# QKV row 0's mean from two partial sums, and a new order of the first loads

## The chip, the cores and the metric

The kernel runs on one core of one Trainium2 chip. Its time is the device time of one execution in microseconds (us), and the median of several runs is compared. A core has TensorE (PE, matrix products into PSUM; its weight loads are listed as PEld), VectorE (DVE), ScalarE (ACT), GpSimd (POOL) and SyncE (SP). Each engine works through its own instructions in order; they wait for each other through semaphores. SyncE and ScalarE each have a queue through which they start DMA transfers; in the profile ScalarE's is q10 and SyncE's q1.

## The reference, cut to what matters

One layer norm feeds two branches, whose results are added to the input: a dilated sliding-window attention (32 heads of 18, 8 keys at distance 2), and a gated feed-forward network.

```python
x = A_x                                    # 1 x 2048 x 576, bf16
xn = _layernorm(x, axis=-1)                # (x - mean) / sqrt(var + 1e-5)
return x + _A_ref(xn, A_wqkv, A_wo) + _B_ref(xn, B_w_gate, B_w_up, B_w_down)

# _A_ref: qkv = x @ wqkv (576 x 1728); for each position s and head h
#   logits over keys s, s-2, ..., s-14 (masked below 0), softmax, weighted sum of v; then @ wo
# _B_ref: (silu(x @ w_gate) * (x @ w_up)) @ w_down, with 4608 hidden columns
```

## The kernel before, in words

The 2048 tokens are 16 row tiles ("rows" 0 to 15) of 128 tokens each, one token to a partition. The kernel has three stretches, one after the other on TensorE: the QKV products of all 16 rows (the first 60 us or so), then for four blocks of four rows the gate and up products (`g_pair`, `g_evac`) and the down and output products (`d_half`, `d_out`). The attention's elementwise work runs on VectorE beside it, from a queue of pieces with written costs (`Filler`). Nothing of this is touched by the change; what it touches is the beginning.

A product needs its operand transposed, with the 576 columns on partitions. They are five slices of 128, the last one padded from 64 columns to 128 by repeating columns 512 to 575. For rows 0 and 1 TensorE itself transposes (`transp_pe`, against an identity matrix), slice by slice into PSUM, and `copy_pt` copies the result to SBUF. `xT_of` names the place: for row 0 the scratch `xcT` (tile PP), for other rows their columns of `xnT`. From row 2 on `transp_halves` or a transposing DMA does it.

The weights `wqkv` come as four slices of 128 rows (`load_w` 0 to 3, 442 KB each) and a rest of 64 rows (`load_w` 4, two transfers of half the columns each); x rows 0 to 3 one at a time (`load_x`, 147 KB each), and later rows in blocks of four. In the profile they go by the tiles that share their memory: x rows are `wd<-in_A_x_dram`, weight slices `hT<-in_A_wqkv_dram`.

Row 0 is treated in a way of its own, so that TensorE need not wait for its variance. Its columns are centered only (`ln_center`, x minus mean, on VectorE; `ln_center_pad`, the padding, on GpSimd); the product is made from that, and the division by the standard deviation is done when the product leaves PSUM (`p_evac` with r = 0 multiplies by `rstd`). The mean comes from `ln_stats(0)`: two BN_STATS over half a row each (`ln_half`) and an aggregate (`ln_aggr`), which give mean and variance. For the feed-forward branch row 0 is also normalized in full later on (`ln_apply(0)` into `xn0`, transposed by a DMA, `transp_dma(0)`). Row 1 is normalized right away: `ln_stats(1)`, `ln_sqrt(1)` on ScalarE, `ln_recip(1)` and `ln_apply(1)` on VectorE, with a padding on GpSimd.

The schedule is written by hand: each engine executes in the order in which the lines at the end (L477 on) issue its instructions. For the first rows this order is, on TensorE: eleven warm-up matmuls on constants (`warm_pe(10, 1)`; ten of 512 columns and one of 128), row 0's five transposes, row 0's products with slices 0, 1 and half of 2 (`p_whole(0, t, ...)`, four matmuls of 432 columns to a slice), row 1's first three transposes, the rest of slice 2, row 1's last two transposes, row 1's products with slice 0 (into the banks `u`), row 0's slice 3 and rest (`p_row0_rest`), and then `p_row(1, ...)`, into which row 2's transposes are inserted.

PSUM has eight banks. `warm_ps` (also `pt1`), `pa`, `pb` and the four banks `t` take seven; of `u` the first is the eighth, and the others take over `pt1`, `pa` and `pb` after their contents have been copied out.

On SyncE's queue a transfer waits for an earlier one where it reuses its semaphore: eight are used in turn, so that the ninth load waits for the landing of the first.

The lines that matter most for the steps below:

```python
477    warm_pe(10, 1)
479    ln_stats(0)
481    ln_center(0, 0, P)
489    ln_stats(1)
492    ln_recip(0)
493    ln_apply(0)
504    copy_pt(nc.vector.tensor_copy, 1, (2,), pa)
```

Of the kernel before, what the change touches and what calls it, by code (L numbers as in the profile page):

```python
# [10 lines left out]
f32 = mybir.dt.float32  # L11
ACT = mybir.ActivationFunctionType
ALU = mybir.AluOpType
AX = mybir.AxisListType
# [3 lines left out]
P = 128  # L18
H, DH, W, DIL = 32, 18, 8, 2
D = H * DH  # L20
HALF = D // 2
# [4 lines left out]
DPAD = KT * P  # L26
# [44 lines left out]
def kernel(  # L71
# [11 lines left out]
    nc = tc.nc  # L83
# [9 lines left out]
    const = ctx.enter_context(tc.tile_pool(name="const", bufs=1))  # L93
# [19 lines left out]
    PP = big.tile([P, 2, RT * D], bf16, name="PP")  # L113
# [30 lines left out]
    def load_x(eng, j):  # L144
        eng.dma_start(xc_b[0][:, j:j + 1, :], x_v[:, j:j + 1, :])

    def load_w(eng, kt):
        if kt < 4:
            eng.dma_start(wqkv[:, kt, :], A_wqkv[kt * P:(kt + 1) * P, :])
        else:  # L150
            for i in range(2):
                eng.dma_start(wqkvr[64 * i:64 * i + 64, :], A_wqkv[4 * P:D, 2 * G * i:2 * G * (i + 1)])

    load_x(nc.scalar, 0)
    load_x(nc.sync, 1)
    load_w(nc.scalar, 1)
    load_w(nc.sync, 0)
    make_identity(nc, ident[:])
    load_w(nc.sync, 2)
    load_x(nc.sync, 2)  # L160
# [8 lines left out]
    pt1 = wp[:].bitcast(bf16)  # L169

    def warm_pe(n, m):
        one = lambda shape: nc.const_aps.tensor(1.0, shape, bf16)
        for i in range(n):
            nc.tensor.matmul(wp[:].rearrange("p (a b) -> p a b", b=P), one([P, P]), one([P, 4, P]),  # L174
                             start=True, stop=True)
        for i in range(m):
            nc.tensor.matmul(wp[:, 0:P], one([P, P]), one([P, P]), start=True, stop=True)  # L177
# [18 lines left out]
    def new_ps(name):  # L196
        return ps.tile([P, 512], f32, name=name, tag="ps")


    ln = {}  # L200

    def ln_open(c):
        mv = lns.tile([P, 4, 2], f32, name="mv")
        rstd = lns.tile([P, 4], f32, name="rstd")
        ln[c] = (xc_b[c], xn_b[c % 2], mv, rstd)

    sums = {}

    def ln_half(r, k):
        c, j = divmod(r, 4)  # L210
        xc, xn, mv, rstd = ln[c]
        if k == 0:
            sums[r] = lns.tile([P, 2, 6], f32, name="stats")
        nc.vector.bn_stats(sums[r][:, k, :], xc[:, j, k * HALF:(k + 1) * HALF])  # L214

    def ln_aggr(r):
        c, j = divmod(r, 4)
        nc.vector.bn_aggr(ln[c][2][:, j, :], sums[r][:].rearrange("p c s -> p (c s)"))

    def ln_stats(r, n=1):  # L220
        for i in range(r, r + n):
            ln_half(i, 0)
            ln_half(i, 1)
            ln_aggr(i)

    def ln_sqrt(r, n=1):
        c, j = divmod(r, 4)
        xc, xn, mv, rstd = ln[c]
        nc.scalar.activation(rstd[:, j:j + n], mv[:, j:j + n, 1], ACT.Sqrt, bias=eps_t[:], scale=1.0)

    def ln_recip(r, n=1):
        c, j = divmod(r, 4)
        rstd = ln[c][3]
        nc.vector.reciprocal(rstd[:, j:j + n], rstd[:, j:j + n])

    def ln_apply(r):
        c, j = divmod(r, 4)
        xc, xn, mv, rstd = ln[c]
        dst = xn[:, j] if r else xn0
        nc.vector.tensor_scalar(dst[:, 0:D], xc[:, j], mv[:, j, 0:1], rstd[:, j:j + 1],  # L240
                                op0=ALU.subtract, op1=ALU.mult)
        if r < 2:
            nc.gpsimd.tensor_scalar(dst[:, D:DPAD], xc[:, j, 512:D], mv[:, j, 0:1], rstd[:, j:j + 1],
                                    op0=ALU.subtract, op1=ALU.mult)
        else:
            nc.vector.tensor_copy(dst[:, D:DPAD], dst[:, 512:D])

    def ln_center(r, lo=0, hi=D):
        c, j = divmod(r, 4)
        xc, xn, mv, rstd = ln[c]  # L250
        nc.vector.tensor_scalar(xn[:, j, lo:hi], xc[:, j, lo:hi], mv[:, j, 0:1], None, op0=ALU.subtract)

    def ln_center_pad(r):
        c, j = divmod(r, 4)
        xc, xn, mv, rstd = ln[c]
        nc.gpsimd.tensor_scalar(xn[:, j, D:DPAD], xc[:, j, 512:D], mv[:, j, 0:1], None, op0=ALU.subtract)

    def transp_pe(r, kts, pt):
        c, j = divmod(r, 4)
        xn = ln[c][1]  # L260
        for i, kt in enumerate(kts):
            nc.tensor.transpose(pt[:, i * P:(i + 1) * P], xn[:, j, kt * P:(kt + 1) * P], ident[:])  # L262

    def xT_of(r):
        return xcT if r == 0 else xnT[:, :, r * P:(r + 1) * P]

    def copy_pt(eng, r, kts, pt):
        eng(xT_of(r)[:, kts[0]:kts[-1] + 1, :],
            pt[:, 0:len(kts) * P].rearrange("p (k t) -> p k t", t=P))

    def new_pt():
        return ps.tile([P, 8 * P], bf16, name="pt", tag="ps")

    def transp_halves(r):


        c, j = divmod(r, 4)
        xn = ln[c][1]
        pt = [new_ps("pt") for half in range(2)]
        for kt in range(KT):  # L280
            for half in range(2):
                rows = slice(64 * half, 64 * half + 64)
                nc.tensor.matmul(pt[half][:, kt * 64:(kt + 1) * 64], xn[rows, j, kt * P:(kt + 1) * P],  # L283
                                 ident[rows, rows], start=True, stop=True)
        for half, eng in enumerate((nc.scalar.copy, nc.vector.tensor_copy)):
            lo = r * P + 64 * half
            eng(xnT[:, :, lo:lo + 64], pt[half][:, 0:KT * 64].rearrange("p (k t) -> p k t", t=64))  # L287
# [11 lines left out]
    def p_mm(t, g, kt, half, r, start, stop):  # L299
        rows = slice(0, P) if half is None else slice(64 * half, 64 * half + 64)  # L300
        return nc.tensor.matmul(t[g][:, 0:G], xT_of(r)[rows, kt, :], w_at(g, kt, rows),  # L301
                                start=start, stop=stop)

    def p_whole(r, t, kt, gs=range(NG)):
        for g in gs:
            p_mm(t, g, kt, None, r, kt == 0, False)
# [6 lines left out]
    def fence_after(mm):  # L313
        f = nc.gpsimd.engine_nop()
        tc.add_manual_dep(f.ins, mm.ins.name, SYNC, reason="first half done")
        return f

    def fence_before(mm, f):
        tc.add_manual_dep(mm.ins, f.ins.name, SYNC, reason="banks change row tiles")

    def p_row(r, between=None, at=(0, 1), t=None):


        done = t is not None
        t = t or [None] * NG
        fence = {}
        for swap in range(2):
            for i in range(2):
                for kt in (0, 1, 2, 3) if swap else (0, 4, 1, 2, 3):
                    if done and kt == 0:  # L330
                        continue
                    for half in range(2):
                        g = i + 2 * (half ^ swap)
                        if t[g] is None:
                            t[g] = new_ps("qkv_ps")
                        mm = p_mm(t, g, kt, half, r, swap == 0 and kt == 0, swap == 1 and kt == 3)
                        if swap == 0 and kt == 3 and half == 1:
                            fence[i] = fence_after(mm)
                        if swap and kt == (1 if done else 0) and half == 0:
                            fence_before(mm, fence[i])  # L340
                    if swap and (i, kt) == at and between is not None:
                        between()
        return t
# [130 lines left out]
    def turn(r):  # L474
        return lambda: transp_halves(r)

    warm_pe(10, 1)  # L477
    ln_open(0)
    ln_stats(0)
    ln_center_pad(0)  # L480
    ln_center(0, 0, P)
    ln_sqrt(0)
    pa, pb = new_pt(), new_pt()
    transp_pe(0, (0,), pa)
    ln_center(0, P, D)
    transp_pe(0, range(1, KT), pb)
    copy_pt(nc.scalar.copy, 0, (0,), pa)
    copy_pt(nc.scalar.copy, 0, (1, 2), pb)
    ln_stats(1)
    ln_sqrt(1)  # L490
    copy_pt(nc.scalar.copy, 0, (3, 4), pb[:, 2 * P:])
    ln_recip(0)
    ln_apply(0)
    ln_recip(1)
    ln_apply(1)

    t = [new_ps("qkv_ps") for g in range(NG)]
    p_whole(0, t, 0)
    p_whole(0, t, 1)
    p_whole(0, t, 2, (0, 1))  # L500
    transp_pe(1, (0, 1), pt1)
    transp_pe(1, (2,), pa)
    copy_pt(nc.scalar.copy, 1, (0, 1), pt1)
    copy_pt(nc.vector.tensor_copy, 1, (2,), pa)
    p_whole(0, t, 2, (2, 3))
    transp_pe(1, (3, 4), pb)
    copy_pt(nc.scalar.copy, 1, (3, 4), pb)
    u = [None] * NG
# [11 lines left out]
    load_gu(0)  # L520
    transp_dma(0)

    p_row(1, turn(2), (0, 2), u)
    ln_aggr(3)
    p_evac(1, u, (0, 1, 2), dve=(1, 2))
    ln_sqrt(3)
# [8 lines left out]
    t = p_row(2, turn(3))  # L535
# [6 lines left out]
    t = p_row(3, turn(4))  # L542
# [10 lines left out]
    for r in range(4, R):  # L553
        t = p_row(r)
# [92 lines left out]
    for tt in range(NTT):  # L647
# [29 lines left out]
        for sub in range(0, RT, 2):  # L677
            t, fence = {}, {}
# [36 lines left out]
```

## Time and profile before

| what | us |
|---|---|
| three runs | 503.34, 503.36, 504.67 (median 503.36) |
| the profiled execution | 503.82 |
| its span | 502.0 |
| PE busy | 498.1 (99%) |
| VectorE busy | 329.0 (66%) |
| ScalarE busy | 200.5 (40%) |
| GpSimd busy | 2.6 (1%) |
| the QKV matmuls (L301) in the chain | 11% of the span |
| the warm-up matmuls (L174) in the chain | 1% of the span |

The profile is of one execution. Its times are counted from the start of the span. A line of the timeline gives the start, the length, the engine (SPq and ACTq are the parts that issue DMAs), the line of the kernel, the operation, the tiles and shapes, the number of instructions merged in the line, and in brackets how long the engine had been idle and what ended that. A matmul's length includes its way through the array, so matmuls overlap; the pace is the distance between starts. The chain is followed back from the last instruction of the program, at each step to what released it, and its lines give start, length and what ran.

### The profile page before, as it was taken

To read this page: it belongs to the slowest core of one execution; us is meant where nothing else is said; L and a number is where in the kernel's file an instruction comes from. 1 tells how busy PE (TensorE), PEld (TensorE's weight loads), DVE (VectorE), ACT (ScalarE), POOL (GpSimd) and SP (SyncE) were. 2 spreads that over 40 slices of the span, in tenths; PEclk is the share of its full clock that TensorE was granted. 3 is DMA by queue.
4 is the path that set the end of the run, shared out by engine and by line. 5 is a ranking of instruction groups with operands and counts; after the bars stand their busy time and mean duration, and the time that the engine had idled before them with its cause. 6 is when DMAs were issued, how large, how long until landed. Compare 5 with 4: busy or idle time off the path is not lost.

```text
span 502.0 us, 13267 instructions
## 1 busy us (share of the span) xinstructions
PE 498.1 (99%) x5795; PEld 330.5 (66%) x5795; DVE 329.0 (66%) x478; ACT 200.5 (40%) x415; POOL 2.6 (1%) x9
## 2 busy tenths in 40 slices
PE   9999999999999999999999999999999999999997
PEld 4666655555799755555899655555999555557996
DVE  5888598898999698999898139995980222221001
ACT  4756657644400255554300445557000454553000
POOL 2000000000000000000000000000000000000000
PEclk9999999999999999999999999999999999999999
DMA  8889988789921045536621154465600335453100
GB/s 313 219 206 228 307 280 280 220 273 309 233 82 61 25 136 193 191 106 225 161 69 43 29 185 146 139 189 157 136 25 14 100 114 178 155 177 38 29 14 25
DMA packets 77186, 75.42 MB, mean 150 GB/s; under 512 B 22708, under 2 KB 72528, under 8 KB 77128
## 3 DMA queue, kind: packets, MB, share of 16 engines
q1 hardware_dynamic: 76840, 73.98, 49.7%
q8 instruction: 45, 0.74, 0.6%
q10 hardware_dynamic: 288, 0.59, 0.4%
q14 instruction: 13, 0.11, 0.1%
HBM read 58.76 MB, written 5.90 MB: 129 GB/s over the span
## 4 chain that ended last, share of the span: by engine, by line
PE 99%; DVE 0%; issue 0%
PE g_ps L601 56%; PE d_ps L630 32%; PE qkv_ps L301 11%; PE warm_ps L174 1%; PE pt L262 0%; DVE ot L644 0%; PE pt L283 0%; PE warm_ps L262 0%; PE warm_ps L177 0%
## 5 line engine op out<-in xcount | busy, mean ns | idle before, releaser
L601 PE MATMUL g_ps<-xnT,gu 64*128 64x512 bf16 x2592 | 280.4, 376 | 0.0
L601 PEld LDWEIGHTS <-gu 64*128 64x128 bf16 x2592 | 147.7, 94 | 131.3
L612 ACT ACTIVATE sg<-g_ps 128x512 bf16<-128x512 f32 x144 | 87.3, 606 | 156.6 <-PE g_ps L601 156.6
L630 PE MATMUL d_ps<-wd,hT 64*128 64x288 bf16 x2304 | 146.9, 283 | 0.0
L630 PEld LDWEIGHTS <-hT 64*128 64x128 bf16 x2304 | 131.3, 94 | 10.5
L614 DVE TENSOR_TENSOR hT<-sg,uc 128x512 bf16<-128x512 bf16 x144 | 60.0, 418 | 93.8 <-ACT uc L613 93.6
L613 ACT CAST uc<-g_ps 128x512 bf16<-128x512 f32 x144 | 85.2, 592 | 0.0
L414 DVE TENSOR_REDUCE PP<-PP 128x64 f32<-128x1152 bf16 x64 | 84.9, 1345 | 0.4
L301 PE MATMUL qkv_ps<-hT,xnT 64*128 64x432 bf16 (+1 forms) x536 | 50.2, 343 | 0.0
L409 DVE TENSOR_TENSOR PP<-QO,Kr 128x2304 bf16<-128x2304 bf16 (+1 forms) x35 | 43.5, 1249 | 7.2 <-DMA Kr<-hT 6.9
L642 DVE TENSOR_TENSOR ot<-d_ps,xr 128x288 bf16<-128x288 f32 x30 | 12.3, 451 | 51.1 <-PE d_ps L630 51.1
L441 DVE TENSOR_TENSOR PP<-Vr,A 128x2304 bf16<-128x2304 bf16 (+1 forms) x35 | 43.2, 1250 | 0.4
L301 PEld LDWEIGHTS <-xnT 64*128 64x128 bf16 (+1 forms) x536 | 30.1, 94 | 18.5 <-ACT xnT L287 0.4
L446 DVE TENSOR_TENSOR PP<-PP 128x2304 bf16<-128x2304 bf16 x24 | 32.5, 1353 | 0.3
L612 ACT ACT_TABLE_LOAD x5 | 6.4, 1283 | 47.3 <-PE g_ps L601 47.2
L630 PE MATMUL d_ps<-wo,xnT 64*128 64x288 bf16 x288 | 23.4, 283 | 0.0
L363 ACT CAST hT<-qkv_ps 128x288 bf16<-128x288 f32 (+2 forms) x58 | 21.2, 428 | 0.5 <-DMA kv_d<-hT 0.5
L630 PEld LDWEIGHTS <-xnT 64*128 64x128 bf16 x288 | 16.4, 94 | 1.2
L434 ACT ACTIVATE PP<-PP 128x1024 f32<-128x1024 f32 x4 | 4.2, 1057 | 31.2 <-DVE PP L430 31.2
L644 ACT CAST ot<-d_ps 128x288 bf16<-128x288 f32 x1 | 0.4, 399 | 38.8 <-PE d_ps L630 38.8
L363 ACT CAST QO<-qkv_ps 128x432 bf16<-128x432 f32 (+1 forms) x30 | 12.3, 410 | 7.4 <-PE qkv_ps L301 7.4
L214 DVE BATCH_NORM_STATS2 stats<-wd 128x6 f32<-128x288 bf16 x32 | 12.9, 444 | 2.9 <-DMA wd<-in_A_x_dram 2.6
(53 smaller groups left out, 91.3 us busy)
## 6 DMA issues: line engine op xcount, KB each, us to landing
gu<-in_B_w_gate_dram SPq DMA_DIRECT2D x36, 512.0 KB, 3.8
gu<-in_B_w_up_dram SPq DMA_DIRECT2D x36, 512.0 KB, 5.1
wd<-in_B_w_down_dram SPq DMA_DIRECT2D x9, 576.0 KB, 6.0
kv_d<-hT SPq DMA_DIRECT2D x5, 576.0 KB, 6.4
gu<-in_B_w_gate_dram SPq DMA_DIRECT2D x36, 64.0 KB, 4.7
gu<-in_B_w_up_dram SPq DMA_DIRECT2D x36, 64.0 KB, 4.4
xr<-in_A_x_dram SPq DMA_DIRECT2D x8, 288.0 KB, 5.1
out_dram<-ot SPq DMA_DIRECT2D x16, 144.0 KB, 1.8
```

What stands on the lines that cost most here:

```text
L214: nc.vector.bn_stats(sums[r][:, k, :], xc[:, j, k * HALF:(k + 1) * HALF])
L301: return nc.tensor.matmul(t[g][:, 0:G], xT_of(r)[rows, kt, :], w_at(g, kt, rows), start=start, stop=stop)
L363: (nc.vector.tensor_copy if n in dve else nc.scalar.copy)(*parts[n])
L409: nc.vector.tensor_tensor(prod[:, a:b], QO[:, RT * tt + a:RT * tt + b, :], Kr[:, s:s + b - a, :], op=ALU.mult)
L414: nc.vector.tensor_reduce(L[:, w, rs], prod[:, rs].rearrange("p r (h d) -> p r h d", d=DH), axis=AX.X, op=ALU.add)
L441: nc.vector.tensor_tensor(dst[:, a:b], Vr[:, s:s + b - a, :].rearrange("p r (d h) -> p r d h", h=H), A[:, w, a:b].unsqueeze(2).to_broadcas ...
L446: nc.vector.tensor_tensor(dst, acc, pv, op=ALU.add)
L601: mm = nc.tensor.matmul(ring_ps[j][b][:], gu[rows, slot, k, fc], xnT[rows, kt, tok], start=(swap == 0 and kt == 0), stop=(swap == 1 and kt ...
L612: nc.scalar.activation(sg[:], t[0][:], ACT.Silu)
L613: nc.scalar.copy(uc[:], t[1][:])
L614: nc.vector.tensor_tensor(hT[:, ch * FC + j, :], sg[:], uc[:], op=ALU.mult)
L630: mm = nc.tensor.matmul(t[sub][h][:, 0:HALF], a[rows], w[rows, h * HALF:(h + 1) * HALF], start=(swap == 0 and n == 0), stop=(swap == 1 and ...
```

## The change

- The first loads change place. x row 0 goes on SyncE's queue and weight slice 0 alone on ScalarE's; SyncE's queue then has x row 1, slices 1 and 2, x row 2, slices 3 and 4 and x row 3. Before, ScalarE's queue had x row 0 and slice 1; SyncE's began with x row 1 and slice 0.
- Row 0's mean is computed by itself (`ln_mean0`): ScalarE copies the first half of the row to scratch and takes along the sum, VectorE sums the second half, and a one-column operation on VectorE adds the two and multiplies by 1/576. `ln_center` and `ln_center_pad` read this mean.
- Row 0's statistics (`ln_half(0, 0)`, `ln_half(0, 1)`, `ln_aggr(0)`, `ln_sqrt(0)`) are issued later, in between and after those of row 1, and `ln_recip(0)` and `ln_apply(0)` come after `ln_apply(1)`.
- ScalarE's third copy of row 0's transposes comes ahead of `ln_sqrt(1)`.
- One 512-column warm-up matmul is dropped (nine instead of ten).
- Three of the four matmuls of row 0's slice 2 come ahead of row 1's transposes, instead of two.
- The copy of row 1's slices 0 and 1 is split in two.
- Row 2's transposes come one step (two matmuls) earlier in `p_row(1, ...)`.

```diff
--- before.py
+++ after.py
@@ -151,10 +151,10 @@
             for i in range(2):
                 eng.dma_start(wqkvr[64 * i:64 * i + 64, :], A_wqkv[4 * P:D, 2 * G * i:2 * G * (i + 1)])
 
-    load_x(nc.scalar, 0)
+    load_x(nc.sync, 0)
+    load_w(nc.scalar, 0)
     load_x(nc.sync, 1)
-    load_w(nc.scalar, 1)
-    load_w(nc.sync, 0)
+    load_w(nc.sync, 1)
     make_identity(nc, ident[:])
     load_w(nc.sync, 2)
     load_x(nc.sync, 2)
@@ -205,6 +205,14 @@
         ln[c] = (xc_b[c], xn_b[c % 2], mv, rstd)
 
     sums = {}
+    part = const.tile([P, 2], f32, name="part")
+    mean = const.tile([P, 1], f32, name="mean")
+
+    def ln_mean0():
+        xc = ln[0][0]
+        nc.scalar.activation(PP[:, 1, 0:HALF], xc[:, 0, 0:HALF], ACT.Copy, accum_out=part[:, 0:1])
+        nc.vector.tensor_reduce(part[:, 1:2], xc[:, 0, HALF:D], axis=AX.X, op=ALU.add)
+        nc.vector.tensor_scalar(mean[:], part[:, 0:1], part[:, 1:2], 1.0 / D, op0=ALU.add, op1=ALU.mult)
 
     def ln_half(r, k):
         c, j = divmod(r, 4)
@@ -248,12 +256,12 @@
     def ln_center(r, lo=0, hi=D):
         c, j = divmod(r, 4)
         xc, xn, mv, rstd = ln[c]
-        nc.vector.tensor_scalar(xn[:, j, lo:hi], xc[:, j, lo:hi], mv[:, j, 0:1], None, op0=ALU.subtract)
+        nc.vector.tensor_scalar(xn[:, j, lo:hi], xc[:, j, lo:hi], mean[:], None, op0=ALU.subtract)
 
     def ln_center_pad(r):
         c, j = divmod(r, 4)
         xc, xn, mv, rstd = ln[c]
-        nc.gpsimd.tensor_scalar(xn[:, j, D:DPAD], xc[:, j, 512:D], mv[:, j, 0:1], None, op0=ALU.subtract)
+        nc.gpsimd.tensor_scalar(xn[:, j, D:DPAD], xc[:, j, 512:D], mean[:], None, op0=ALU.subtract)
 
     def transp_pe(r, kts, pt):
         c, j = divmod(r, 4)
@@ -474,35 +482,39 @@
     def turn(r):
         return lambda: transp_halves(r)
 
-    warm_pe(10, 1)
+    warm_pe(9, 1)
     ln_open(0)
-    ln_stats(0)
+    ln_mean0()
     ln_center_pad(0)
     ln_center(0, 0, P)
-    ln_sqrt(0)
     pa, pb = new_pt(), new_pt()
     transp_pe(0, (0,), pa)
     ln_center(0, P, D)
     transp_pe(0, range(1, KT), pb)
     copy_pt(nc.scalar.copy, 0, (0,), pa)
     copy_pt(nc.scalar.copy, 0, (1, 2), pb)
+    copy_pt(nc.scalar.copy, 0, (3, 4), pb[:, 2 * P:])
     ln_stats(1)
     ln_sqrt(1)
-    copy_pt(nc.scalar.copy, 0, (3, 4), pb[:, 2 * P:])
+    ln_half(0, 0)
+    ln_recip(1)
+    ln_apply(1)
+    ln_half(0, 1)
+    ln_aggr(0)
+    ln_sqrt(0)
     ln_recip(0)
     ln_apply(0)
-    ln_recip(1)
-    ln_apply(1)
 
     t = [new_ps("qkv_ps") for g in range(NG)]
     p_whole(0, t, 0)
     p_whole(0, t, 1)
-    p_whole(0, t, 2, (0, 1))
+    p_whole(0, t, 2, (0, 1, 2))
     transp_pe(1, (0, 1), pt1)
     transp_pe(1, (2,), pa)
-    copy_pt(nc.scalar.copy, 1, (0, 1), pt1)
+    copy_pt(nc.scalar.copy, 1, (0,), pt1)
+    copy_pt(nc.scalar.copy, 1, (1,), pt1[:, P:])
     copy_pt(nc.vector.tensor_copy, 1, (2,), pa)
-    p_whole(0, t, 2, (2, 3))
+    p_whole(0, t, 2, (3,))
     transp_pe(1, (3, 4), pb)
     copy_pt(nc.scalar.copy, 1, (3, 4), pb)
     u = [None] * NG
@@ -520,7 +532,7 @@
     load_gu(0)
     transp_dma(0)
 
-    p_row(1, turn(2), (0, 2), u)
+    p_row(1, turn(2), (0, 1), u)
     ln_aggr(3)
     p_evac(1, u, (0, 1, 2), dve=(1, 2))
     ln_sqrt(3)
```

## The prediction

> **What bounds the kernel now.** I read the page's busy table first, then its chain, then the same chain in order of time, and last the first 14 us as a timeline, engine by engine.
>
> ```profile
> PE 498.1 (99%) x5795; PEld 330.5 (66%) x5795; DVE 329.0 (66%) x478; ACT 200.5 (40%) x415; POOL 2.6 (1%) x9
> PE 99%; DVE 0%; issue 0%
> ```
>
> TensorE (PE) is busy for 99% of the span and is 99% of the chain that ended last, so a microsecond by which its stream shifts is a microsecond of the time. The change touches the first 13 us alone. The chain there:
>
> ```profile
> 0.76 4.42 PE warm_ps L174 x10
> 5.18 0.11 PE warm_ps L177
> 5.29 0.21 PE pt L262
> 5.50 0.02 issue
> 5.52 0.61 PE pt L262 x4
> 6.13 2.25 PE qkv_ps L301 x10
> 8.37 0.11 PE warm_ps L262 x2
> 8.48 0.06 PE pt L262
> 8.54 0.37 PE qkv_ps L301 x2
> 8.91 0.11 PE pt L262 x2
> 9.02 3.86 PE qkv_ps L301 x32
> ```
>
> The eleven warm-up matmuls compute nothing: PE's real work starts with row 0's transposes at 5.2. From the first QKV matmul (starts 6.06) it hardly pauses, so I follow one milestone: the start of slice 3 of row 0 (`p_whole(0, t, 3)`), 9.69 now. By the timeline nothing after it waits for long (0.10 us at 10.42, 0.13 us at 13.6), so a shift there reaches the end. What leads up to it, in the timeline of all engines:
>
> ```profile
> 3.81 0.82 DVE L214 BATCH_NORM_STATS2 stats<-wd 128x6 f32<-128x288 bf16 x2 [2.63 <-DMA wd<-in_A_x_dram]
> 4.66 0.21 DVE L218 BATCH_NORM_AGGREGATE mv<-stats 128x2 f32<-128x12 f32 x1
> 4.90 0.56 DVE L251 TENSOR_SCALAR wd<-wd,mv 128x128 bf16<-128x128 bf16 x2
> 5.54 0.27 ACT L268 COPY PP<-pt 128x128 bf16<-128x128 bf16 x1 [0.34 <-PE pt L262]
> 6.13 0.43 SPq L165 DMA_DIRECT2D wd<-in_A_x_dram  x1
> 8.58 0.23 DVE L268 COPY xnT<-pt 128x128 bf16<-128x128 bf16 x1 [1.11 <-PE pt L262]
> ```
>
> Row 0 lands at 3.81 (VectorE had waited 2.63 us for it). Statistics take to 4.90, where the centering starts. The copy of the first transposed slice ends at 5.81 and the transposes stream until 5.92, but the first QKV matmul waits until 6.06 for weight slice 0; SyncE's second block load, which waits for that same slice, goes at 6.13. At 8.58 the last row shows slack: VectorE has idled 1.11 us when it copies row 1's third slice out of PSUM.
>
> **Part 1, the loads.** DMA queues q10 (ScalarE) and q1 (SyncE), between 2.4 and 2.8 us, then between 3.6 and 4.8:
>
> ```profile
> q10 hardware_dynamic: 57, 0.06, 50.2%
> q1 hardware_dynamic: 53, 0.06, 42.6%
> ...
> q1 hardware_dynamic: 75, 0.26, 53.5%
> q10 hardware_dynamic: 73, 0.25, 50.0%
> ...
> wd<-in_A_x_dram ACTq DMA_DIRECT2D x1, 144.0 KB, 3.1
> wd<-in_A_x_dram SPq DMA_DIRECT2D x1, 144.0 KB, 3.2
> ```
>
> With both queues loaded, each gets the same number of packets, whatever their size. Packets are rows: 1152 bytes of x (51 ns of an engine each: q1's 42.6% of 16 engines' 0.4 us over 53 packets), 3456 of a weight slice (about 136 ns, in the same way from the second pair). Now x row 0 shares the engines with x row 1: 8 packets of each on each of 16 engines, 16 x 51 = 0.82 us. After the change it shares them with slice 0: 8 x (51 + 136) = 1.50 us, 0.68 more. It also moves to SyncE's queue, whose row took 3.2 us instead of 3.1. Row 0's landing goes from 3.81 to 0.72 + 3.2 + 0.68 = 4.60. Bounds: 3.9 (the smaller packets lose nothing) and 4.75. Slice 0 gains: it finishes beside row 0, near 4.6 instead of 6.02, and its wait at 6.06 is gone. Slices 2 to 4 have the same bytes ahead of them as before. SyncE issues two loads more and one less; at 0.44 to 0.6 us an issue its eighth, which waits for row 0's landing (3.80 now), starts at 4.6, with over 1 MB still queued, so nothing runs dry. ScalarE issues one load less (0.46), hidden before the landing.
>
> **Part 2, the mean.** Removed ahead of the centering: two BN_STATS and the aggregate, 3.81 to 4.90 = 1.10 us. Added, on two engines side by side: VectorE's reduction of 288 values, 0.34 us by the row of 1152 in 1345 ns, 0.44 by BN_STATS over the same 288; ScalarE's copy of 288, 0.43 us (CAST of 288) to 0.50 (ACTIVATE of 288), and reading out its sum, which no row shows: nothing, or 0.20 (the one-column ACTIVATE `warm`, nearest), up to 0.29 (the one-column ACTIVATE `rstd`). I take 0.43 + 0.20 + 0.04 for the handover, then one column on VectorE, 0.19 start to start (reciprocal to its user, 6.85 to 7.04). Centering starts 0.86 after the landing (0.65 to 1.05), 0.24 sooner than 1.10. Call its start C: 4.60 + 0.86 = 5.46 against 4.90.
>
> **Part 3, PE up to the first QKV matmul.** The first transpose starts C + 0.31 = 5.77 and the matmuls C + 1.03 = 6.49, against 6.06: 0.43 late. The dropped warm-up (0.43) ends PE's warm-up at 4.66; PE then idles 1.1 us instead of 0.13, and the drop gains nothing.
>
> **Part 4, the new order on VectorE and ScalarE.** Distances start to start from the trace of before: bn(1) at C + 0.48 and + 0.85, aggregate + 1.32, then half of row 0's statistics + 1.45. ScalarE's three copies + 0.63, + 1.26, + 1.56, and sqrt(1) + 1.87. recip(1) + 2.22, apply(1) + 2.41, second half of row 0 + 2.76, aggregate + 3.24, sqrt(0) + 3.48, recip(0) + 3.83, apply(0) + 4.03, and only then the copy of row 1's third slice, + 4.38 to + 4.60. That copy frees the PSUM bank `pa`; by the trace of before the second matmul of row 1's slice 0 (9.14) is the one that waits for a VectorE semaphore, and this copy is the only candidate I see. It now starts at C + 4.65 = 10.11 instead of 9.14. On ScalarE row 1's copies stand behind sqrt(0): C + 3.75 to + 4.0 for the first, within that bound; splitting it costs 0.17 of ScalarE, also within. Moving one matmul (0.18) ahead of row 1's transposes is an exchange on PE; they would be reached near 8.7, when row 1 (C + 2.84 = 8.3) and its pad on POOL (0.64 more, needed by the last two alone) are there.
>
> So the milestone moves from 9.69 to 10.11 + 3 x 0.183 = 10.66: **+0.97 us**, of which 0.56 is C and the rest the order. Row 2's transposes are moved two matmuls up; VectorE has row 2 ready at C + 4.38 + 2.40 = 12.25, PE comes at 12.72 + 0.97 - 0.18 = 13.5, no wait. The transposing DMA of row 0 waits for apply(0), and its pad on POOL, at about 10.3 now; it went at 11.6, behind SyncE's gu loads: hidden.
>
> **The sum.** The profiled execution took 503.82 (span 502.0 and 1.82 around it), 0.46 above the median of the runs, so it is 504.79 there, and 503.36 + 0.97 = **504.3** for the median. (0.3%, 1.5 us, is about what a measurement of this kernel can tell from no change.)
>
> **Rivals.**
> *The clock comes later (slower).* Early matmuls run at half the later pace: the 512-column warm-ups 0.43 us apart, QKV matmuls of 432 columns 0.36 apart at 6.38, and 0.183 apart from 6.9 on, 6 us after PE began. If PE's new idle stretch makes that run-up start over at 5.77, the fast pace comes at 11.8: eleven matmuls at 0.36 (6.49 to 10.45), three transposes 0.32, one matmul, two transposes 0.21, and most of row 1's slice 0 slow bring the milestone to 12.26: +2.57, 505.9. For it: the idle stretch is over 1 us, where the run-up of before had three pauses of 0.1 to 0.2. Against it: the granted clock of the windows reads 1.00 throughout and shows no such state. It decides once the fast pace comes after about 8 us. [...]
> *Row 0 isn't delayed.* The small packets pass the large ones: landing 3.92, C = 4.78, milestone 9.98: +0.29, 503.65. With the cheapest mean (0.65) it is +0.08. Against it: the equal packet counts.
> *Faster by over 0.3%.* PE would have to start QKV at 4.6, the very end of its warm-ups, and VectorE's chain of part 4 not to hold it. Against it: 1.4 us is all there is between warm-up's end and 6.06. At best, without the `pa` wait and the delay, about 503.1.
>
> **How the numbers follow.** My forecast 0.54 (503.9 to 504.7); no delay 0.16; clock 0.28; faster 0.02. Of the forecast a tenth lies past 504.87, from the upper bounds of landing and mean. Slower 0.33, same 0.65, faster 0.02. Range: from 503.2, below the undelayed row, to 505.9, the clock rival.
>
> **What would show it.** Row 0's landing by VectorE's first wait: 4.6, or 3.9. Centering 0.86 after it. First QKV matmul at 6.5. Row 1's third copy after apply(0), near 9.8, and PE's wait for it. The spacing of QKV matmuls before and after 7 us. I am wrong if the two queues don't alternate, if another operation than that copy frees the bank, or if the clock's run-up restarts.

## The result, and the profile after

The changed kernel takes 505.47 us (median of 8 executions, 504.56 to 507.34), the kernel before 503.51 (8 executions, 503.32 to 504.67). The ratio is 1.0044, with a 95% interval of 1.0026 to 1.0061. That is slower, by 2.0 us. Not only the median moved: the executions of the kernel before lie within 1.4 us, those of the changed one within 2.8.

The page of the changed kernel's profiled execution (505.23 us, span 503.4), its busy line of TensorE and its chain by engine:

```profile
PE 497.4 (99%) x5794; PEld 282.6 (56%) x5794; DVE 329.7 (65%) x480; ACT 201.0 (40%) x418; POOL 2.7 (1%) x9
PE 97%; DMA 2%; DVE 1%; ACT 0%; issue 0%
```

TensorE is no longer 99% of the chain: some 2% are transfers and 1% VectorE, which TensorE waited for at two places. (The shares say how long the chain runs through what was waited for; TensorE itself stood still for much less.) The first place is in the timeline of the first 11 us (start, length, engine, line, what ran; in brackets the idle time before):

```profile
0.76 4.00 PE L174 MATMUL warm_ps<-const-bfloat16-1.0 128*128 128x512 bf16 x9 [0.76 <-PEq L711]
...
4.82 0.44 ACT L213 ACTIVATE PP<-wd 128x288 bf16<-128x288 bf16 x1 [2.17 <-DMA wd<-in_A_x_dram]
4.82 0.45 DVE L214 TENSOR_REDUCE part<-wd 128x1 f32<-128x288 bf16 x1 [3.64 <-DMA wd<-in_A_x_dram]
5.17 0.19 ACT L213 ACTIVATION_READ_ACCUMULATOR PP<-wd 128x1 f32 x1
5.38 0.21 DVE L215 TENSOR_SCALAR mean<-part 128x1 f32<-128x1 f32 x1
...
5.63 0.56 DVE L259 TENSOR_SCALAR wd<-wd,mean 128x128 bf16<-128x128 bf16 x2
...
5.95 0.70 PE L270 MATMUL pt<-ident,wd 128*128 128x128 bf16 x5 [1.08 <-DVE wd L259]
...
6.53 2.18 PE L309 MATMUL qkv_ps<-hT,PP 128*128 128x432 bf16 x11
...
9.70 0.22 DVE L276 COPY xnT<-pt 128x128 bf16<-128x128 bf16 x1
...
9.97 0.71 PE L309 MATMUL qkv_ps<-hT,xnT 128*128 128x432 bf16 x3 [0.28 <-DVE xnT L276]
...
10.52 1.36 PE L309 MATMUL qkv_ps<-hT,PP 128*128 128x432 bf16 x8
```

Row 0 lands at 4.82 instead of 3.81. The new mean takes 0.81 us from there to the centering at 5.63 (it was 1.10). TensorE has ended its warm-ups (starts at 4.12 and 4.55 are its last) and idles 1.08 us after the last one's end, 1.4 us from start to start, until the first transpose at 5.95. Later it waits another 0.28 us in the middle of row 1's slice 0, for VectorE's copy at 9.70; by the pace, 0.18 us from start to start, its second matmul there comes 0.45 us late (9.97 instead of 9.52). The start of slice 3 of row 0, the prediction's milestone, is at 10.52 (9.69 before).

The second place is far from the change. Between 128 and 140 us TensorE waits for the first transposing DMA of the attention's result (who waited for whom, total, times, longest):

```profile
PEld L642 <- DMA xnT<-QO: 0.8, 1, 0.8
PE d_ps L642 <- DMA xnT<-QO: 0.5, 1, 0.5
```

The matmul that follows starts 0.67 us later than its pace would have it. In the trace of before there is no such wait. The books of the two spans close with these: 0.83 us at the milestone, 0.13 less up to the end of the QKV stretch (the wait of 0.13 us at 13.6 in the kernel before is gone), 0.67 in the wait near 134 us: 1.37 of the 1.38 us between the spans (502.03 and 503.41).

The 9.69 of before is itself a late one. In that trace the QKV matmuls still start 0.31 and 0.36 us apart up to 6.73, and by the clock's record the full clock was granted at 6.76. Two later traces with the same first 14 us (e8 and e11) had it at 3.94 and 4.41, all QKV matmuls at the fast pace, and the milestone at 9.26 and 9.30. Against these the changed kernel, whose QKV matmuls are all at the fast pace too, is 1.2 us late instead of 0.83.

That explains the profiled execution. It doesn't explain the slowest ones, which take 2 us more than it. For them every execution's mean granted clock is of use (from the fastest to the slowest):

```
changed kernel, us:      504.56 505.23 505.27 505.33 505.61 506.64 507.30 507.34
mean granted clock:       1.000  1.000  0.999  0.999  0.997  0.997  0.996  0.996
```

The four slowest are those that lost clock: 0.3 to 0.4% of 505 us is 1.5 to 2.0 us. It is not a plain sum: 505.61 has the same 0.997 as 506.64 and lies only 0.3 us above executions that lost nothing.

### The profile page after: what moved, and what is told of

It is laid out like the page before. It is cut to its first block, busy times and chain, and to the rows that moved or that the text cites. A ratio compares the mean times of both kernels' runs of the same rounds, so it can differ in the third digit from the quotient of the medians.

```text
span 503.4 us, 13270 instructions
## 1 busy us (share of the span) xinstructions
PE 497.4 (99%) x5794; PEld 282.6 (56%) x5794; DVE 329.7 (65%) x480; ACT 201.0 (40%) x418; POOL 2.7 (1%) x9
## 4 chain that ended last, share of the span: by engine, by line
PE 97%; DMA 2%; DVE 1%; ACT 0%; issue 0%
PE g_ps L613 56%; PE d_ps L642 31%; PE qkv_ps L309 10%; DMA xnT<-QO 1%; DMA wd<-in_A_x_dram 1%; ACT PP L276 0%; DVE wd L259 0%; ACT PP L213 0%; ACT rstd L237 0%; DVE ot L656 0%; PE pt L291 0%; DVE wd L248 0%; DVE A L248 0%; PE pt L270 0%; DVE stats L222 0%
## 5 line engine op out<-in xcount | busy, mean ns | idle before, releaser
L613 PEld LDWEIGHTS <-gu 64*128 64x128 bf16 x2592 | 126.1, 94 | 153.0
L642 PEld LDWEIGHTS <-hT 64*128 64x128 bf16 x2304 | 112.2, 94 | 29.7
L309 PEld LDWEIGHTS <-xnT 64*128 64x128 bf16 (+1 forms) x536 | 25.9, 94 | 23.2 <-issue 0.5
L642 PEld LDWEIGHTS <-xnT 64*128 64x128 bf16 x288 | 13.9, 94 | 4.4 <-DMA xnT<-QO 0.8
```

What stands on the lines that cost most here:

```text
L613: mm = nc.tensor.matmul(ring_ps[j][b][:], gu[rows, slot, k, fc], xnT[rows, kt, tok], start=(swap == 0 and kt == 0), stop=(swap == 1 and kt ...
L642: mm = nc.tensor.matmul(t[sub][h][:, 0:HALF], a[rows], w[rows, h * HALF:(h + 1) * HALF], start=(swap == 0 and n == 0), stop=(swap == 1 and ...
```

## The experiments

The theory after the first profile: three things add up. Row 0 lands late because its packets alternate with the larger ones of slice 0; the order on VectorE holds TensorE 0.3 us; and the pause after the warm-ups costs the fast clock in part of the executions. The rival to the last: landing and order are all, and the spread is chance. e1 to e4 ran on one chip with the kernel before beside them, and so did e5 to e8, e9 and e10, and e11 and e12. In the table "slice 3" and "lands" are from the kernel's one trace.

| run | median (lowest to highest), us | ratio to before, 95% | lands | slice 3 |
|---|---|---|---|---|
| before, first trace | 503.51 (503.32 to 504.67) | - | 3.81 | 9.69 |
| changed | 505.47 (504.56 to 507.34) | 1.0044 (1.0026 to 1.0061) | 4.82 | 10.52 |
| e1 12 warm-ups | 504.53 (504.03 to 505.76) | 1.0015 (1.0006 to 1.0023) | 4.82 | 10.37 |
| e2 loads as before | 504.25 (503.66 to 504.98) | 1.0011 (1.0002 to 1.0019) | 3.58 | 9.29 |
| e3 copy ahead of normalization | 506.16 (504.17 to 507.38) | 1.0042 (1.0027 to 1.0056) | 4.80 | 11.37 |
| e4 before, 7 warm-ups | 504.64 (503.37 to 506.63) | 1.0012 (1.0000 to 1.0024) | 3.81 | 9.12 |
| e5 loads as before, 10 warm-ups | 504.25 (503.89 to 504.68) | 1.0006 (0.9997 to 1.0015) | 4.08 | 10.00 |
| e6 row 0 on ScalarE's queue | 505.82 (one) | - | 5.01 | 11.80 |
| e7 e3 with 12 warm-ups | 504.47 (504.28 to 505.32) | 1.0008 (0.9996 to 1.0019) | 4.85 | 10.23 |
| e8 before, xr late | 503.69 (503.37 to 504.18) | 0.9995 (0.9986 to 1.0004) | 3.67 | 9.26 |
| e9 built from the findings | 506.25 (505.64 to 506.77) | 1.0046 (1.0032 to 1.0059) | 3.32 | 11.46 |
| e10 changed again | 505.12 (504.48 to 506.01) | 1.0027 (1.0018 to 1.0037) | 4.82 | 10.53 |
| e11 before again | 504.09 (one) | - | 3.68 | 9.30 |
| e12 changed, xr late | 504.64 (504.52 to 505.67) | 1.0018 (1.0007 to 1.0029) | 4.91 | 10.62 |

The kernel before had medians of 503.64, 503.88, 503.65 and 503.69 beside these four groups. In e9 slice 3 comes behind four more matmuls of row 1 than in the others, so its 11.46 isn't comparable.

### e1: fill the pause

```diff
-    warm_pe(9, 1)
+    warm_pe(12, 1)
```

> The changed kernel with 12 long warm-up matmuls instead of 9 and nothing else: they end near 5.97, where row 0's first transpose starts (5.95), so the pause of 1.3 us on TensorE is filled. Theory (that pause costs the fast clock in many executions; the rest of the loss is row 0's later landing and the order on VectorE, 0.83 us at the start of slice 3): the executions draw together near 504.3, every one with a mean granted clock of 0.999 or more. Rival (the clock has no part in it, the whole loss of about 2 us lies in landing and order): the median stays within 0.3 of 505.5 and the spread of 2.8 us stays.

Measured: 504.53, no execution with a mean clock below 0.999, and 11 of 12 within 0.85 us. Three warm-up matmuls more, which compute nothing, bring the median to 0.6 to 0.9 us below the two measurements of the changed kernel (505.47, and 505.12 in e10). The chain of e1's first microseconds, in order of time, shows that nothing else moved:

```profile
0.76 5.28 PE warm_ps L174 x12
6.03 0.11 PE warm_ps L177
6.14 0.11 PE pt L270
...
9.82 0.14 DVE xnT L276
9.96 0.04 issue
10.01 3.37 PE qkv_ps L309 x28
```

The transposes start where they did and the stream goes on behind VectorE's copy at 10.01, as in the changed kernel (9.97). What went away is the executions of 506.6 us and more, all of which had lost clock in the changed kernel. Over all runs a mean clock of 0.997 or less is found six times, and only in kernels with the pause: four times in the changed kernel, once in e6 and once in e12. In the 92 executions of the kernel before beside e1 to e12, and in those of e1, e2, e5, e7, e8 and e11, none lies below 0.999.

### e4: make such a pause in the kernel before

```diff
-    warm_pe(10, 1)
+    warm_pe(7, 1)
```

> The kernel before with 7 long warm-up matmuls instead of 10: TensorE pauses from 3.8 to 5.2, 1.4 us, and nothing waits for the dropped matmuls. Theory (a pause of over 1 us after the warm-ups costs the fast clock in part of the executions): median 504.2 to 505.5, a spread of 2 us or more, granted clock down to 0.996 in some executions. Rival (the pause costs nothing): 503.5 as the kernel before, clock 0.999 or more.

Measured: a median 1.0 us above that of the kernel before, and executions from 503.37 to 506.63. In the traced one slice 3 starts earlier than ever (9.12): all its QKV matmuls ran at the fast pace (ten in 1.88 us, 2.25 in the first trace of before), as they do with ten warm-ups in e8 and e11. So the pause does not cost in every execution; it opens the spread upwards, for the lowest (503.37) is that of the kernel before beside it (503.34). The mean granted clock, which I had expected to sink to 0.996, stayed at 1.000: as e3 shows, slow time at the start isn't counted in it. That its longer executions had more such half-clock time at the start is argued, for none of them was traced. The interval (1.0000 to 1.0024) just touches no change. So e4 alone proves little; what shows the pause's effect is the traces of e6 and e3 below, e1, which does the opposite to the other kernel, and where the lost clock is found.

### e6: row 0 on the other queue

```diff
-    load_x(nc.sync, 0)
-    load_w(nc.scalar, 0)
+    load_x(nc.scalar, 0)
+    load_w(nc.sync, 0)
```

> The changed kernel with x row 0 on ScalarE's queue and weight slice 0 on SyncE's, so that row 0 keeps its partner and changes its queue. Theory (row 0 is late because its small packets alternate with slice 0's packets of three times the size): it still lands at 4.6 to 4.8. Rival (SyncE's queue is the slower one): it lands at 3.8.

Measured: landing at 5.01, later still than I expected and far from the rival's 3.8; the queue is not the reason, and with the partner of before (e2 and e5) the row lands at 3.58 and 4.08. The page of the changed kernel's DMA between 2.4 and 3.6 us shows the sharing itself (packets, MB, share of the engines' time):

```profile
q10 hardware_dynamic: 67, 0.23, 47.7%
q1 hardware_dynamic: 71, 0.08, 31.7%
```

About equal numbers of packets, 0.23 MB for slice 0 and 0.08 for the x rows.

This trace also caught what the clock does. The table of windows of e6 (length, then busy us and instructions of PE, PEld, DVE, ACT and POOL, granted clock, DMA share, GB/s):

```profile
3.40:5.10 1.70, 0.81 (x5) 0.22 (x3) 0.09 (x1) 0.09 (x1) 0.00 (x0) 1.00 1.03 399
5.10:6.80 1.70, 0.59 (x6) 0.40 (x7) 1.55 (x6) 0.71 (x3) 0.58 (x1) 1.00 1.02 405
6.80:8.50 1.70, 1.70 (x7) 0.69 (x7) 1.56 (x6) 0.84 (x3) 0.48 (x1) 0.51 1.05 407
8.50:10.20 1.70, 1.70 (x6) 0.71 (x5) 1.05 (x4) 0.29 (x1) 0.84 (x2) 0.50 1.10 263
10.20:11.90 1.70, 1.69 (x13) 0.97 (x12) 1.07 (x4) 0.72 (x3) 0.15 (x1) 0.99 1.02 407
```

TensorE had the full clock from 3.4 us on: the spacing of its warm-ups falls from 0.43 to 0.22 us there, so that they end early and the pause grows to 1.92 us. In the 3.4 us up to 6.8 it was busy for 0.81 + 0.59 = 1.40 us, and at 6.8, when it was busy again, the clock fell to half until 10.2: another 3.4 us. In these the QKV matmuls start 0.36 us apart, and 0.18 after it. Half the clock for 3.4 of 504 us is the mean of 0.997 that this execution has, and the 0.996 and 0.997 in the list of the changed kernel's executions are about as much. Slice 3 starts at 11.80, 1.28 later than in the changed kernel's trace, though row 0 landed only 0.19 later.

### e3: the copy ahead of the normalization

```diff
-    ln_recip(0)
-    ln_apply(0)
 ...
     copy_pt(nc.vector.tensor_copy, 1, (2,), pa)
+    ln_recip(0)
+    ln_apply(0)
```

> The changed kernel with row 0's reciprocal and normalization on VectorE behind the copy of row 1's third slice instead of ahead of it. Theory: that copy goes at 8.95 instead of 9.71, the second matmul of row 1's slice 0 no longer waits for it (now 0.28 us idle at 9.70), slice 3 of row 0 starts near 10.07 instead of 10.52: 0.45 us off the time, the pause and the spread unchanged, median near 505.0. Rival (another operation holds the bank): no change of the milestone, median 505.5.

Measured: 506.16, and in the trace slice 3 at 11.37. The expectation failed, and the chain of e3 says why:

```profile
6.84 3.32 PE qkv_ps L309 x11
10.16 0.11 PE warm_ps L270 x2
10.28 0.06 PE pt L270
10.33 0.18 PE qkv_ps L309
10.51 0.11 PE pt L270 x2
10.62 0.01 issue
10.63 3.38 PE qkv_ps L309 x25
```

The eleven matmuls that took 2.18 us in the changed kernel's trace take 3.32 here: they start 0.36 us apart until 9.2 and 0.183 after it. The clock had not become fast before the pause, and by its record became so only at 9.38. In the 3.41 us ahead of that rise (about the distance of the clock's changes in e6) TensorE was busy for 3.39 us; in the 3.41 us before those, which hold the pause, for 2.34, and no rise came. In the changed kernel's trace the rise at 5.1 follows 3.41 us with 3.19 busy, and most of the pause comes after it. That what the pause costs hangs on where it falls against the clock's changes is my estimate from these three traces; that the clock keeps a step of 3.41 us in every execution isn't shown. Note that the windows read a clock of 1.00 here (the number before the last two), so the slow time before the first rise shows in the spacing of the matmuls alone:

```profile
6.80:8.50 1.70, 1.70 (x7) 0.67 (x5) 1.35 (x6) 0.84 (x3) 0.49 (x1) 1.00 1.06 388
```

The wait for VectorE that this run was to remove is gone in this trace (row 1's slice 0 follows without a pause), but nothing can be said of its worth. Nor is the clock all of this execution's 1.6 us over the changed kernel's (spans 505.05 and 503.41): slice 3 is 0.85 late, and the wait near 134 us takes 1.3 us instead of 0.67.

### e7: the same with the pause filled

```diff
-    warm_pe(9, 1)
+    warm_pe(12, 1)
-    ln_recip(0)
-    ln_apply(0)
 ...
     copy_pt(nc.vector.tensor_copy, 1, (2,), pa)
+    ln_recip(0)
+    ln_apply(0)
```

> The changed kernel with 12 long warm-ups and with row 0's reciprocal and normalization behind the copy of row 1's third slice. With the pause filled, the order alone is told: TensorE's wait in the middle of row 1's slice 0 (10.01 with 12 warm-ups) goes, slice 3 of row 0 starts near 10.1 instead of 10.37. Theory: 0.25 us less than with 12 warm-ups alone, median 504.3. Rival (the order on VectorE costs nothing): 504.5.

Measured: slice 3 at 10.23 against 10.37 in e1, ratio 1.0008 against 1.0015, on another chip. The chain now runs through ScalarE, the other half of the new order:

```profile
8.99 0.29 ACT rstd L237
9.28 0.16 ACT xnT L276
9.45 0.05 issue
9.49 3.75 PE qkv_ps L309 x30
```

Row 1's first copy stands behind the square root for row 0 (L237), and that behind VectorE's statistics. So the wait for the copy was real, and behind it waits the next, 0.14 us earlier in the trace. In time, e1 and e7 can't be told apart.

### e2 and e5: the loads as before

```diff
-    load_x(nc.sync, 0)
-    load_w(nc.scalar, 0)
+    load_x(nc.scalar, 0)
     load_x(nc.sync, 1)
-    load_w(nc.sync, 1)
+    load_w(nc.scalar, 1)
+    load_w(nc.sync, 0)
```

> The changed kernel with the first four loads on the queues and in the order of before. Theory: row 0 lands at 3.8 again instead of 4.80, centering starts near 4.65, the pause on TensorE shrinks to about 0.3 us, the first QKV matmul waits for slice 0 at about 6.05, and slice 3 of row 0 starts near 9.5 (9.69 in the kernel before, 10.52 in the changed one): median 503.3 to 503.5, granted clock 0.999 or more in all executions. Rival (the loads aren't what costs; mean and order are): still 505 or more.

> The changed kernel with the first four loads as before and ten long warm-ups again: what is left of the change is the mean and the order. Theory (the fast clock needs an unbroken run-up; in the run with the loads as before and nine warm-ups three pauses of together 1.05 us were left): the pauses shrink to about 0.6 us, slice 3 of row 0 starts near 9.3 to 9.5 (9.69 in the kernel before), median 503.3 to 503.6. Rival (mean and order cost by themselves): 504.2 as with nine.

e5 has `warm_pe(10, 1)` besides. Measured: row 0 lands at 3.58 and 4.08, so the loads explain the landing, and the ratio falls from 1.0044 and 1.0027 (two measurements of the changed kernel) to 1.0011 and 1.0006. But both medians are 504.25, 0.7 above what I expected, and neither is faster than the kernel before, though the mean is 0.29 us shorter. The chain of e5 from its centering on shows the new order holding TensorE, as in the changed kernel:

```profile
8.62 0.02 issue
8.64 0.17 DVE rstd L242
8.81 0.03 issue
8.84 0.43 DVE A L248
9.27 0.14 DVE xnT L276
9.41 0.04 issue
9.46 3.55 PE qkv_ps L309 x29
```

Normalization of row 0 (A, L248), then the copy, then TensorE. In e5 slice 3 starts at 10.00. Row 0 lands 0.27 later than in the first trace of before and the mean is as much shorter, so that the centering starts at 4.90 in both: the 0.31 us at slice 3 are the new order's. For e2, whose trace has slice 3 at 9.29 (9.26 and 9.30 in e8 and e11, which have the kernel before's first 14 us), what lifts the median isn't settled: three pauses of together 1.05 us are left after its warm-ups, and its trace has a wait of 0.3 us near 134 us. That the fast clock needs an unbroken run-up, the guess in e5's theory, no run shows: in the first trace of before it came at 6.76, after three pauses of 0.1 to 0.2 us.

### e8, e11 and e12: the wait near 134 us

```diff
             if ch == NCH - 1:
                 ...
+                for i in (0, 2):
+                    nc.sync.dma_start(xr[:, i:i + 2, :], ...)
 ...
-            if ch == 7:
-                for i in (0, 2):
-                    nc.sync.dma_start(xr[:, i:i + 2, :], ...)
```

e8 makes this edit in the kernel before, e12 in the changed one; e11 is the kernel before, unchanged.

> The kernel before with the residual's row loads (xr) issued behind the transposing DMAs of the attention's result instead of ahead of them; nothing of the first 14 us differs. Theory (TensorE waits near 134 us for the first of those transposes in executions whose transfers run slower; 0 to 1.3 us in the traces): the transposes go over 1 us sooner, the wait is gone, the upper part of the executions (504.1 to 504.9) vanishes, median 503.4 to 503.5. Rival (that wait is chance and not what spreads the executions): spread and median as before, 503.6.

> The kernel before itself, for a second trace of it. Theory (the wait near 134 us for the first transpose of the attention's result hangs on the pace of the transfers in an execution, not on the change): it may show here too, between 0 and 0.7 us. Rival (the change causes it): no wait, as in the first trace. Time 503.3 to 504.9.

> The changed kernel with the xr loads behind the transposes of the attention's result and nothing else. Theory (of the changed kernel's loss about 0.5 us is TensorE's wait near 134 us, 0.67 and 0.54 us in its two traces): no wait there, 0.4 to 0.6 us off: median 504.6 to 504.9 where the changed kernel has 505.1 to 505.5; the clock's part of the spread stays. Rival (the loss is all in the first 14 us): 505.1 to 505.5.

The second trace of the kernel before has the wait too:

```profile
PEld L630 <- DMA xnT<-QO: 0.8, 1, 0.8
PE d_ps L630 <- DMA xnT<-QO: 0.5, 1, 0.5
```

So the change doesn't create it: 0 and about 0.6 us in two traces of the kernel before, 0.67 and 0.54 in two of the changed one. The transposes go out behind loads in SyncE's queue, and how fast these run differs between executions (the 512 KB load of `w_up` ahead of them took 5.4 us to land in the first trace of before, 6.1 in the changed kernel's, 7.9 in e3's). That delays the first transpose in two ways. In the changed kernel's trace and in e11 it is issued no later, against TensorE's own progress, than in the first trace of before (130.8 and 129.8; there 130.1) and lands after 4.8 us instead of 3.4; in e10 and e3 it is issued late (132.1 and 133.6), behind the xr loads, and lands after 3.4 and 3.7. With the xr loads behind them the wait is absent from both traces, but so it is from those of e5, e6 and e7, which have the xr loads ahead. In the kernel before the highest execution falls from 506.42 (of 27) to 504.18 (of 11) and the median by 0.2, which the interval can't tell from nothing. In the changed kernel the executions fall into two groups, seven at 504.52 to 504.64 and four at 505.50 to 505.67, with a median 0.5 to 0.8 below that of the changed kernel. One of the upper four has a mean clock of 0.997, the others 1.000; what lifts those wasn't traced. With the xr loads late in both, the changed kernel's median is 0.95 us above that of the kernel before (504.64 against e8's 503.69, measured on different chips): about what landing and order cost by themselves. The traces don't show that the wait comes more often with the change than without it: 0.3 to 1.3 us in e1, e2 and e3, 0.4 in e4, none in e5, e6 and e7.

### e10: the changed kernel again

No edit.

> The changed kernel itself once more, on the chip of the version built from the findings, for its spread and a second trace. Theory (three groups of executions by what the clock does around the pause: no loss, late, taken back for 3.4 us): executions between 504.5 and 507.4, those with a mean granted clock of 0.996 to 0.997 the slowest of them; median 505.5, 1.5 to 2 us above the kernel before.

Measured: 505.12, 1.5 us above the kernel before, and the same milestone to 0.01 us (10.53). None of the 12 executions has a mean clock below 0.999 this time, against four of eight in the first measurement. How often the clock is lost differs from one measurement to the next. The ratios 1.0044 and 1.0027 may differ by that; their intervals overlap.

### e9: a version built from the findings

```diff
-    load_x(nc.sync, 0)
-    load_w(nc.scalar, 0)
+    for eng, p0 in ((nc.sync, 0), (nc.scalar, 64)):
+        eng.dma_start(xc_b[0][p0:p0 + 64, 0:1, :], x_v[p0:p0 + 64, 0:1, :])
+    load_w(nc.scalar, 0)
 ...
-    warm_pe(9, 1)
+    warm_pe(8, 3)
```

with the order of rows 0 and 1 that its expectation tells, and the xr loads late.

> A version built from what the runs before showed: x row 0 in two halves, one first on each queue (nothing larger beside it), slice 0 behind it on ScalarE's; the mean as in the change; eight long and three short warm-ups; row 1's transposes ahead of row 0's slice 2, its slice 1 ahead of row 0's slice 3; on VectorE the copy of row 1's third slice ahead of row 0's later statistics, sqrt(0) behind ScalarE's copies; the xr loads behind the attention's transposes. Theory: row 0 lands near 3.4, centering 0.82 later, first QKV matmul near 5.2 instead of 6.06, the start of slice 3 near 9.5 with four matmuls of row 1 more (0.73) already done: 0.6 to 0.9 us off, median 503.0. Rival (the transfers of slices 1 and 2 set the pace whatever comes first): 503.6 to 503.9 as the kernel before.

Measured: 506.25, the slowest median of all. Row 0 lands at 3.32 and the first QKV matmul starts at 5.35, as hoped, and after four of them TensorE stands still for 1.7 us, in the timeline of e9:

```profile
5.35 1.01 PE L310 MATMUL qkv_ps<-hT,PP 128*128 128x432 bf16 x4
...
8.06 0.89 PE L310 MATMUL qkv_ps<-hT,PP 128*128 128x432 bf16 x4 [1.71 <-DMA hT<-in_A_wqkv_dram]
```

Slice 1 landed at 8.0 instead of 6.4. Between 3.6 and 6.0 us the transfers moved 264 to 291 GB/s in this trace and 382 in e10's on the same chip. That the two loads of 64 rows each at the head of the queues slowed those behind them isn't shown. The rival was right in that slice 1's transfer holds TensorE, but it had expected no loss against the kernel before.

## Why the prediction was right or wrong

The forecast was 504.3, within 0.3% of no change; the time is 505.47, a ratio of 1.0044. It lies in the range (503.2 to 505.9), on the side to which I had given 0.33. The steps up to the milestone came true within 0.2 us; the median lies 1.2 us above the forecast for reasons that the sum doesn't contain, and that the range holds it is owed to the clock rival, whose price is the range's end. That is in part luck.

- **The landing** was right in kind: 4.60 predicted, 4.82 measured, and e6 (5.01, beside slice 0 on the other queue) and e2 (3.58, beside row 1) show that it is the partner on the engines, not the queue. (The two windows that the prediction shows hold packets of like size on both queues, 1152 bytes in the first and 3456 in the second. Equal numbers at unlike sizes are measured in the changed kernel's window, 67 and 71 with 0.23 and 0.08 MB, and between 2.8 and 3.2 us of the kernel before, 65 and 66 with 0.10 and 0.07.) The last 0.2 us were missed: the 16 engines finish row 0 between 4.04 and 4.80, and the slowest sets the landing.
- **The mean** was right: 0.86 predicted, 0.81 measured. The readout of ScalarE's sum, which no row showed, is an instruction of its own of 0.19 us (0.20 taken from the one-column ACTIVATE).
- **The first QKV matmul** was predicted at 6.49 and came at 6.53; the pause of TensorE ahead of the first transpose was seen, with 1.1 us.
- **The order on VectorE**: the wait for the copy that frees the bank was predicted at 10.11 and came at 9.97; the milestone at 10.66 and 10.52. Of the shift of 0.83, the order's part is about the 0.31 that e5 shows with the centering at 4.90.
- **The base of the shift.** The sum added the 0.97 to the median of before, but counted it from the milestone 9.69 of an execution that the clock had made late. From the 9.26 and 9.30 of e8 and e11 the predicted 10.66 is 1.4 us, which would have made the forecast 504.7 to 504.8.
- **"A shift there reaches the end"** was right for the shift, but for the 0.13 us taken up at 13.6, and wrong as a statement that nothing else comes between. TensorE waits near 134 us for a transposing DMA, in executions of both kernels. One trace without that wait didn't show how thin its margin is. It is 0.67 of the profiled execution's 1.38.
- **The clock** is the term that was mis-sized. I made it a rival that either comes or doesn't, with a chance of 0.28; it comes in some executions of the same kernel and not in others, so a share of it belonged in the forecast. What I held against it, that the windows read 1.00 throughout, was void, for e3 reads 1.00 while its matmuls run at half the pace (0.36 us apart against 0.183). Nor did a run-up of 6 us start over in e6: there the clock changes at 3.4, 6.8 and 10.2, so the fast pace is back at 10.2 and not at the 11.8 of my rival. The milestones of e6 and e3, 11.80 and 11.37, are 2.1 and 1.7 past the 9.69 of before, less than my 2.57.
- **"The drop gains nothing"**, said of the tenth warm-up, was too kind. In e1 three more of these empty matmuls are worth 0.6 to 0.9 us, and none of its 12 executions has a mean clock below 0.999, where four of the changed kernel's first eight have 0.996 or 0.997 (and none of e10's 12). What the tenth alone would have been worth in the changed kernel no run tells.
- **Row 0 isn't delayed** and **faster by over 0.3%** fell: the first with the landing, the second with every run.

What stays open: the share of executions in which the clock is lost (four of eight, none of twelve, one of eleven in e12), why e2's median is 0.6 above that of before while its milestone is no later than in e8 and e11, what lifts three executions of e12 by 1 us without lost clock, and what slowed e9's transfers.

## What to carry to other kernels

A load that the start of a kernel waits for should have small company. In the changed kernel's trace the two queues moved 67 and 71 packets between 2.4 and 3.6 us; by their shares of the engines a row of 1152 bytes took 86 ns there and the row of 3456 beside it 137, where two rows of 1152 side by side took 51 and 56 in the kernel before, and row 0 landed at 4.82 instead of 3.81. Warm-up matmuls should reach to the first real one: with twelve, which end where the first transpose starts, the median is 504.53 (e1), with nine 505.47 and 505.12. A pause behind them can come with slow microseconds (half the clock for 3.4 us in e6), and does so in some executions only (a mean clock of 0.997 or less in four of the changed kernel's first eight, in none of e10's 12), which one profile doesn't show. And a mean that is 0.3 us shorter is worth nothing where later work on the same engine, put ahead of a copy that frees a bank, takes the time back (0.31 us at slice 3 in e5).

## What the hardware showed that I had not expected

- In e6 TensorE lost a clock that it had been given: full from 3.4 us, 1.40 us busy of the next 3.4, half from 6.8 to 10.2. In the changed kernel's trace no such loss followed a pause of 1.08 us (1.92 in e6): there, by the clock's record, it rose at 5.1, inside the pause, and stayed up (eleven matmuls in 2.18 us). In e9 it stayed up too, with 1.70 us busy of 3.41.
- The slow time before the first rise isn't in the granted clock that the views show: e3 reads 1.00 while QKV matmuls start 0.36 us apart. By the record that first rise comes anywhere from 3.4 (e6) to 9.38 us (e3), in three traces of the kernel before's first 14 us at 3.94, 4.41 and 6.76.
- ScalarE's sum costs an extra instruction of 0.19 us beside its ACTIVATE of 0.44.
- In one trace (e9) two loads of half the partitions at the head of the two queues went with 264 to 291 GB/s behind them, where e10, with full-height loads, had 382. That the halves are the cause isn't shown.
